# A new order for the first stage of an attention kernel with two feed-forward blocks: pieces, ring places and PSUM banks

## The chip, the cores and the metric

The kernel runs on one core of a Trainium2 chip. The metric is the device time of one execution in microseconds (us); for the kernel before it is the median of three runs. Beside these stands one profiled execution, whose trace is read below.

## What is computed

From `q`, `k`, `v` of shape (4, 8, 576, 64), all float32, attention is computed within chunks of 64 positions; its result, as 2304 tokens by 512, goes through two feed-forward blocks of width 2048.

```python
scores = scale * np.matmul(q_c, k_c.transpose(0, 1, 2, 4, 3))     # chunks of 64
attn = softmax(scores); out = np.matmul(attn, v_c)
x = out.transpose(0, 2, 1, 3).reshape(2304, 512)
r = np.maximum(x @ w_in, 0.0); x = (s * (r * r) + b) @ w_out       # first block
h = x @ w_in2; return (h * np.tanh(softplus(h))) @ w_out2           # second block
```

## The kernel before

The 2304 tokens are 18 tiles of 128, grouped in five blocks of 512, 512, 256, 512 and 512 tokens. The feed-forward width is cut into 16 chunks of 128, four to a group. The kernel has a first stage, which does the attention of all 18 tiles and the first group (four chunks) of the first block, and then a long second stage, in which loops go over the remaining groups of both blocks. Matmuls are done in two words (high and low parts of each number), three products for one.

The first stage is written out by hand as one string, `START`. Each word is a piece, and the pieces are issued in that order; a piece goes to the queue of its engine, so that each engine meets its own pieces in the order of the string. A word is a name, the index of a tile, weight or step, after a dot the place in an SBUF ring, and after @ the PSUM banks. The names that matter here:

- Loads, all on SP's queue: `dq`, `dk`, `dv` bring a tile of q, k or v (256 KB each; tiles 4 and 13 come as two halves). `W` brings a 512 KB weight: 0, 1, 3, 5 are the input weights of chunks 0 to 3, and 2, 4, 6, 7 their output weights. `sb` brings two scalars. From tile 8 on, q and k share a ring of six places: a load into a place waits until TensorE has read what lay there.
- TensorE (PE in the profile): `K` and `Q` transpose a loaded tile (4 matmuls, L248); `S` makes the scores (L271, 32 rows in the profile); `T` transposes the softmax (L248); `X` multiplies with v (L313). `I` and `J` are the two halves of a feed-forward input product (6 matmuls each, L342), `O` and `P` those of an output product (L378). There are 20 feed-forward steps, four for each block. `w5@6` issues five matmuls of zeros (L459; ten rows in the profile) into a bank: filler.
- ScalarE (ACT) and VectorE (DVE): `k`, `q`, `t` copy a transposed tile out of PSUM (ACT); `m`, `e`, `n`, `z` are the softmax; `x`, `y` split the attention's output in two words; `a`, `c`, `d`, `h`, `l` decode a weight; `r`, `u`, `v`, `g`, `o` are the activation. `E` takes a finished sum out of banks 0 to 3 (on ACT for the first sum of a block, L388). `F` and `G` prepare the second stage.

```python
for w in START.split():
    name, i, m, bank = re.fullmatch(r"([a-zA-Z]+)(\d*)(?:\.(\d))?(?:@(\d+))?", w).groups()
    pieces(name, int(i or 0), int(m or 0), int(bank or 0))
```

Of the kernel before, what the change touches and what calls it, by code (L numbers as in the profile page):

```python
# [21 lines left out]
NS = 4  # L22

START = (
# [26 lines left out]
)  # L51

PAIRS = ((0, 1), (3, 4))
# [1406 lines left out]
```

## Time and profile before

| What | us |
|---|---|
| median of 3 runs (lowest, highest) | 814.95 (814.93, 816.12) |
| the profiled execution's own time | 818.31 |
| its span, first to last instruction | 816.5 |
| PE busy in the span | 798.9 (98%) |
| DVE busy, ACT busy | 656.8 (80%), 499.8 (61%) |

The profiled execution has 1.8 us around its span and took 3.4 us more than the median. "Busy" of PE includes filler, and a matmul counts as busy also while the clock is low. Where PE is not busy, the timeline names in brackets how long it stood and what ended the wait.

### The profile page before, as it was taken

Reading aid. Unit: us, or ns where it says so; the run is one execution under the profiler, and the core shown is the slowest. Engines: PE = TensorE matmul, PEld = TensorE weight load, DVE = VectorE, ACT = ScalarE, POOL = GpSimd, SP = SyncE. Lnnn points to the kernel's source line nnn. Section 1 sums busy time; section 2 is a strip of 40 time slices with the busy share of each in tenths; the row PEclk is TensorE's granted clock in tenths of the full one; section 3 lists DMA queues with packets and bytes.
Section 4 is the critical chain, followed back from the end, with each engine's and each line's share of the span. In section 5 each row is a group of like instructions: output and inputs, shape, how many; then the busy total and the mean of one; then the engine's idle time right before and its main releaser. Section 6 shows DMA issues by size and latency. Waiting matters only on the chain.

```text
span 816.5 us, 13885 instructions
## 1 busy us (share of the span) xinstructions
PE 798.9 (98%) x5482; PEld 696.1 (85%) x5482; DVE 656.8 (80%) x1174; ACT 499.8 (61%) x905; POOL 0.7 (0%) x7
## 2 busy tenths in 40 slices
PE   7879999999999999999999999999999999999998
PEld 6767888888888888888888888899899998998997
DVE  5778899968776697757987796899969999889774
ACT  4769767776657486644767364767446563746460
POOL 0000000000000000000000000000000000000000
PEclk9999999999999999999999999999999999999999
DMA  8999622197596543855156440877655757545522
GB/s 199 215 236 264 212 64 81 72 339 259 157 379 240 203 156 140 324 208 204 52 188 243 193 201 3 318 302 255 221 206 192 275 189 261 186 172 212 194 86 104
DMA packets 102049, 163.43 MB, mean 200 GB/s; under 512 B 60000, under 2 KB 80480, under 8 KB 92256
## 3 DMA queue, kind: packets, MB, share of 16 engines
q1 hardware_dynamic: 101984, 162.55, 57.9%
q8 instruction: 43, 0.70, 0.4%
q14 instruction: 22, 0.18, 0.1%
HBM read 127.40 MB, written 35.13 MB: 199 GB/s over the span
## 4 chain that ended last, share of the span: by engine, by line
PE 90%; SPq 4%; DMA 3%; ACT 1%; DVE 1%; issue 0%; DVEq 0%
PE ps L955 38%; PE ps L378 29%; PE ps L987 17%; PE ps L342 5%; SPq L240 3%; DMA qk<-in_k_dram 1%; DMA wraw<-in_moe_w_in_dram 1%; PE ps L248 1%; DMA qk<-in_q_dram 1%; PE ps L313 1%; DVE wdec L158 0%; PE ps L271 0%; ACT ysum L388 0%; ACT wdec L158 0%; ACT r L471 0%
## 5 line engine op out<-in xcount | busy, mean ns | idle before, releaser
L378 PE MATMUL ps<-ghi,w 128*128 128x512 f32 (+1 forms) x512 | 130.0, 371 | 0.0
L955 PE MATMUL ps<-xs,wx 128*128 128x512 f32 (+1 forms) x516 | 121.9, 376 | 0.0
L378 PEld LDWEIGHTS ps<-ghi,w 128*128 128x128 f32 x512 | 91.3, 189 | 15.9
L955 PEld LDWEIGHTS ps<-xs,wx 128*128 128x128 f32 x516 | 90.4, 189 | 15.5
L955 PE MATMUL ps<-xs,w 128*128 128x512 f32 (+1 forms) x384 | 89.3, 370 | 0.0
L158 DVE SCALAR_TENSOR_TENSOR wdec<-wraw,wdec 128x512 uint32<-128x512 uint32 x128 | 87.2, 688 | 1.8
L955 PEld LDWEIGHTS ps<-xs,w 128*128 128x128 f32 x384 | 67.2, 189 | 11.5
L378 PE MATMUL ps<-glo,w 128*128 128x512 f32 (+1 forms) x256 | 75.1, 369 | 0.0
L955 PE MATMUL ps<-xs,wb 128*128 128x512 f32 x288 | 74.6, 391 | 0.0
L158 DVE TENSOR_SCALAR wdec<-wdec 128x512 f32<-128x512 f32 (+1 forms) x128 | 53.3, 423 | 15.9 <-ACT wdec L158 14.8
L955 PEld LDWEIGHTS ps<-xs,wb 128*128 128x128 f32 x288 | 52.7, 188 | 9.8
L1004 DVE TENSOR_TENSOR ysum<-ps,ysum 128x512 f32<-128x512 f32 x76 | 51.4, 687 | 11.7 <-PE ps L987 11.2
L399 DVE TENSOR_TENSOR ysum<-ps,ysum 128x512 f32<-128x512 f32 (+1 forms) x66 | 39.9, 638 | 23.8 <-PE ps L378 23.8
L378 PEld LDWEIGHTS ps<-glo,w 128*128 128x128 f32 x256 | 46.9, 188 | 8.3
L1119 ACT COPY ur<-ps 128x512 f32<-128x512 f32 x40 | 23.5, 587 | 43.2 <-PE ps L955 40.8
L342 PE MATMUL ps<-xhi,w 128*128 128x512 f32 (+1 forms) x160 | 46.7, 375 | 0.0
L987 PE MATMUL ps<-wc,rm 128*128 128x256 f32 x312 | 44.4, 282 | 0.0
L987 PEld LDWEIGHTS ps<-wc,rm 128*128 128x128 f32 x312 | 41.6, 191 | 1.4
L378 PE MATMUL ps<-gr,w 128*128 128x512 f32 (+1 forms) x192 | 42.6, 363 | 0.0
L158 DVE TENSOR_TENSOR w<-wdec,w 128x512 fp32r<-128x512 f32 x50 | 34.2, 686 | 9.9 <-ACT w L158 9.9
L1119 ACT COPY ps<-ps 128x512 f32<-128x512 f32 (+1 forms) x56 | 29.0, 521 | 19.8 <-PE ps L987 10.2
L378 PEld LDWEIGHTS ps<-gr,w 128*128 128x128 f32 x192 | 33.4, 189 | 5.7
(210 smaller groups left out, 1616.6 us busy)
## 6 DMA issues: line engine op xcount, KB each, us to landing
wraw<-in_moe_w_in_dram SPq DMA_DIRECT2D x32, 512.0 KB, 5.7
wraw<-in_moe_w_out_dram SPq DMA_DIRECT2D x32, 512.0 KB, 5.3
xs<-d20t SPq DMA_DIRECT2D x12, 1024.0 KB, 5.1
xs<-d23t SPq DMA_DIRECT2D x12, 1024.0 KB, 4.7
xs<-d13b SPq DMA_DIRECT2D x9, 1024.0 KB, 6.1
xs<-d20b SPq DMA_DIRECT2D x9, 1024.0 KB, 4.9
xs<-d23b SPq DMA_DIRECT2D x9, 1024.0 KB, 6.2
xs<-d10t SPq DMA_DIRECT2D x8, 1024.0 KB, 7.4
```

What stands on the lines that cost most here:

```text
L158: ins = issue(**z)
L240: nc.sync.dma_start(out=t[o:o + n].rearrange("p (h d) -> p h d", h=H), in_=dict(k=k, q=q, v=v)[which][bb, :, ss:ss + n, :].rearrange("h s ...
L248: nc.tensor.transpose(out=p[:, a], in_=src[:, a * P:(a + 1) * P], identity=ident)
L313: nc.tensor.matmul(out=xp[j * CH:(j + 1) * CH, c, a, :], lhsT=at["v", i][r, h * CH:(h + 1) * CH], rhs=at["pt", i][r, 2 * ap + a2, g:g + CH],)
L342: nc.tensor.matmul(out=hp, lhsT=w[:, sl], rhs=r[b][:, a, :], start=(a == 0 and p == 0), stop=(a == KD - 1 and p == 2),)
L378: nc.tensor.matmul(out=acc[m][:, :n] if l == 1 else acc[m], lhsT=w[wi][:, sl] if l == 1 else g[gi][:, sl], rhs=g[gi] if l == 1 else w[wi], ...
L399: nc.vector.tensor_tensor(out=y, in0=a[:, :w], in1=y, op=ALU.add)
L955: nc.tensor.matmul(out=out, lhsT=w[i][:, a * P:(a + 1) * P], rhs=x[j][:, a], start=(begins and a == 0 and p == 0), stop=(ends and a == KD ...
L987: nc.tensor.matmul(out=bank[:, t * n:(t + 1) * n], lhsT=g[u][x][:, (2 * j + t) * P:(2 * j + t + 1) * P], rhs=w[u][y], start=False, stop=(u ...
L1004: nc.vector.tensor_tensor(out=z, in0=bank.rearrange("p (t d) -> p t d", d=n), in1=z, op=ALU.add)
L1119: nc.scalar.copy(out=out, in_=i)
```

## The change

The string `START` is replaced. The pieces are the same apart from the filler: 17 calls of a zero matmul before (in four words), 23 after (in ten). What differs is their order, the ring places and the banks. The first line and its replacement:

```diff
-    "dk2 W0 dq2 w5@6 K2@0 dk3 dq3 a0 k2.0 dq0 w5@6 Q2@0 c0 dk0 dk6 K3@4 dk5 q2.0 dk1 d0 S2@67 k3.1 Q3@2 dq5 dq1 h0 "
...
+    "dk1 w5@6 K1@6 dq1 Q1@4 W0 k1.0 dk3 dq3 q1.0 dq0 w1@6 S1@23 m1.4 a0 e1 c0 n1 d0 w3@6 K3@4 k3.1 w2@6 Q3@1 dq2 w2@6 "
...
```

The loads alone, in queue order up to the k tile 12, and then PE's pieces up to the transposes of that tile:

```
loads before: dk2 W0 dq2 dk3 dq3 dq0 dk0 dk6 dk5 dk1 dq5 dq1 dq6 dq4 dq15 dq9 dk9 dv2 dk10 dk7 dq7 dv3 dv0 dk4 dv1
              dq12 dq8 W1 dq10 dv5 dk17 sb dv6 dk8 dk16 dv7 dk11 dq11 dv4 dq14 dq16 dk12
loads after:  dk1 dq1 W0 dk3 dq3 dq0 dq2 dk0 dk2 dq9 dk6 dq6 dq5 dk5 dv1 dv3 dk9 dv0 dk4 dq4 dv2 W1 dq7 dq10 dk7 dv5
              dk10 dk8 dv6 dq8 dv7 dq11 dv4 dk12 | sb W3 dk11 W2 dv9 dq12 dq16 W5 dk15 dk13
PE before: w5 K2 w5 Q2 K3 S2 Q3 Q0 S3 K0 w2 S0 w5 Q5 K1 K5 K6 T2 Q1 Q6 S1 Q4 T3 S6 Q15 K9 X2 S5 Q9 K10 K7 T0 S9 X3
           Q7 T1 X0 K4 T6 S7 X1 S4 Q12 Q8 I0 T5 Q10 J0 K17 S10 X6 X5 K8 K16 I3 T4 J3 T7 K11 X4 S8 X7 Q14 Q11 K12
PE after:  w5 K1 Q1 w1 S1 w3 K3 w2 Q3 w2 Q0 S3 Q2 w2 K0 w2 K2 S0 T1 Q9 S2 w3 Q6 w2 Q5 K6 K5 S6 w1 T3 T0 S5 X1 K9 T2
           X0 S9 K4 Q4 X3 X2 T5 S4 I0 J0 Q7 K7 T6 Q10 X5 S7 K10 I3 J3 K8 Q8 X6 S10 T7 T4 Q11 X7 X4 S8 T9 K12
```

On SP's queue the change shows at the k tile 12. Before, the rows from the v tile 6 (`v_86`) to the k tile 12, the last row (rows of 64 are half tiles):

```order
L240 DMA v_86<-in_v_dram 128x8x64
L240 DMA qk<-in_k_dram 128x8x64 x2
L240 DMA v_86<-in_v_dram 128x8x64
L240 DMA qk<-in_k_dram 128x8x64
L240 DMA qk<-in_q_dram 128x8x64
L240 DMA v_86<-in_v_dram 64x8x64 x2
L240 DMA qk<-in_q_dram 128x8x64 x2
L240 DMA qk<-in_k_dram 128x8x64
```

After, from the v tile 6 to the k tile 12 and on to the weight `W3`:

```order
L240 DMA v_86<-in_v_dram 128x8x64
L240 DMA qk<-in_q_dram 128x8x64
L240 DMA v_86<-in_v_dram 128x8x64
L240 DMA qk<-in_q_dram 128x8x64
L240 DMA v_86<-in_v_dram 64x8x64 x2
L240 DMA qk<-in_k_dram 128x8x64
L438 DMA s_sb<-in_moe_s_dram 128x1
L439 DMA b_sb<-in_moe_b_dram 128x1
L146 DMA wraw<-in_moe_w_in_dram 128x4x256
```

Four q and k loads stood between the v tiles 6 and 4 and two q loads between the v tile 4 and the k tile 12; now it is two and none, and the two scalars come behind the k tile 12.

On PE at the same tile, before: the transposes of the q tiles 14 and 11, the k tile 12 and the q tile 16 in one row (x16), then those of the softmax of tile 9 (`e`) and the product `I2` on the second block's tokens:

```order
L248 MATMUL ps<-ident,e_87 128x128 x4
L248 MATMUL ps<-ident,qk 128x128 x4
L313 MATMUL ps<-room,v_86 64x64 x16
L271 MATMUL ps<-kt,qt 64x64 x16
L313 MATMUL ps<-room,v_86 64x64 x16
L248 MATMUL ps<-ident,qk 128x128 x16
L248 MATMUL ps<-ident,e 128x128 x4
L342 MATMUL ps<-xhi_701,w 128x512 x2
```

After: the last row of transposes from `qk` is that of the k tile 12; in front stand the products of tiles 7 and 4 with v, the scores of tile 8 and the softmax of tile 9, behind it `I1`:

```order
L248 MATMUL ps<-ident,e_87 128x128 x8
L248 MATMUL ps<-ident,qk 128x128 x4
L313 MATMUL ps<-room,v_86 64x64 x32
L271 MATMUL ps<-kt,qt 64x64 x16
L248 MATMUL ps<-ident,e 128x128 x4
L248 MATMUL ps<-ident,qk 128x128 x4
L342 MATMUL ps<-xhi_621,w 128x512 x2
```

The transposes of the q tiles 14 and 16 have moved behind the k tile 12, and the softmax of tile 9 in front of it.

## Rows read from the trace of the kernel before

**Rows 1.** Busy time by stretch: each engine's us and count, PE's clock, DMA share, GB/s.
```profile
0.00:20.00 20.00, 15.09 (x168) 13.11 (x169) 10.10 (x20) 8.25 (x13) 0.74 (x7) 0.95 0.85 199
20.00:40.00 20.00, 17.72 (x402) 15.05 (x400) 15.50 (x31) 14.51 (x27) 0.00 (x0) 0.97 0.95 222
40.00:60.00 20.00, 15.01 (x266) 12.63 (x265) 15.51 (x31) 13.77 (x26) 0.00 (x0) 1.00 0.89 225
60.00:80.00 20.00, 20.00 (x217) 16.39 (x216) 16.38 (x33) 17.55 (x33) 0.00 (x0) 1.00 0.97 254
80.00:100.00 20.00, 18.32 (x244) 15.27 (x243) 16.51 (x32) 15.71 (x30) 0.00 (x0) 1.00 0.76 251
100.00:171.60 71.60, 71.60 (x595) 60.73 (x594) 67.74 (x113) 52.75 (x100) 0.00 (x0) 1.00 0.28 96
171.60:816.50 644.90, 641.13 (x3600) 562.96 (x3598) 515.04 (x918) 377.28 (x680) 0.00 (x0) 1.00 0.57 207
```

**Rows 2.** PE's waits over the span: us in total, times, longest.
```profile
PE ps L248 <- DMA qk<-in_q_dram: 4.1, 4, 2.4
PE ps L248 <- DMA qk<-in_k_dram: 4.0, 6, 1.5
PE ps L313 <- DMA v<-in_v_dram: 1.7, 1, 1.7
PE ps L248 <- ACT kt L256: 1.2, 2, 0.6
PE ps L271 <- ACT ysum L388: 1.1, 1, 1.1
```

**Rows 3.** Timeline of PE: start, length, what, count, idle before; filler and early stops.
```profile
1.05 2.50 PE L459 MATMUL ps<-zero 128*128 128x128 f32 x10 [1.05 <-DVE zero L863]
...
4.67 2.34 PE L459 MATMUL ps<-zero 128*128 128x128 f32 x10
...
13.78 1.38 PE L459 MATMUL ps<-zero 128*128 128x128 f32 x10
17.53 3.30 PE L248 MATMUL ps<-ident,qk 128*128 128x128 f32 x16 [2.36 <-DMA qk<-in_q_dram]
```

**Rows 4.** Timeline of PE, the later stops for a load, and what follows the last.
```profile
34.17 0.63 PE L248 MATMUL ps<-ident,qk 128*128 128x128 f32 x4 [0.81 <-DMA qk<-in_k_dram]
...
41.19 0.63 PE L248 MATMUL ps<-ident,qk 128*128 128x128 f32 x4 [1.04 <-DMA qk<-in_q_dram]
...
45.94 1.16 PE L313 MATMUL ps<-room,v 64*64 64x64 f32 x64 [1.67 <-DMA v<-in_v_dram]
...
49.16 0.63 PE L248 MATMUL ps<-ident,qk 128*128 128x128 f32 x4 [1.46 <-DMA qk<-in_k_dram]
...
57.28 1.06 PE L248 MATMUL ps<-ident,qk 128*128 128x128 f32 x8 [0.82 <-DMA qk<-in_k_dram]
...
60.01 0.62 PE L342 MATMUL ps<-xhi,w 128*128 128x512 f32 x2
...
61.38 0.62 PE L342 MATMUL ps<-xhi,w 128*128 128x512 f32 x2
```

**Rows 5.** Timeline of PE: the two last stops of the first stage, and its end.
```profile
81.30 0.66 PE L248 MATMUL ps<-ident,room 128*128 128x128 f32 x4 [0.59 <-ACT kt L256]
...
86.54 1.17 PE L271 MATMUL ps<-kt,qt 64*64 64x64 f32 x60 [1.09 <-ACT ysum L388]
...
171.39 0.61 PE L955 MATMUL ps<-xhi,w 128*128 128x512 f32 x2
```

**Rows 6.** Timeline of ACT: the weight W3 is awaited.
```profile
61.03 0.66 ACT L158 ACTIVATE wdec<-wraw 128x512 f32<-128x512 f32 x1 [0.61 <-DMA wraw<-in_moe_w_in_dram]
```

**Rows 7.** SP's waits before loads, between 30 and 60 us, by what ended them.
```profile
SPq L240 <- PE ps L248: 4.4, 4, 1.9
```

**Rows 8.** Busy time by stretch: after the longest stop, and around the scalars.
```profile
16.00:18.00 2.00, 0.47 (x4) 0.48 (x5) 1.26 (x4) 0.00 (x0) 0.00 (x0) 0.99 0.33 77
18.00:20.00 2.00, 2.00 (x12) 2.00 (x11) 0.55 (x1) 1.12 (x2) 0.00 (x0) 0.50 0.97 219
20.00:22.00 2.00, 2.00 (x14) 2.00 (x13) 1.67 (x5) 1.07 (x2) 0.00 (x0) 0.65 1.03 232
22.00:24.00 2.00, 1.71 (x43) 1.40 (x42) 0.41 (x1) 1.56 (x3) 0.00 (x0) 1.00 0.89 203
...
42.00:44.00 2.00, 2.00 (x38) 1.52 (x40) 1.93 (x4) 1.69 (x4) 0.00 (x0) 1.00 0.21 35
```

50 rows, old and new, of the table START are left out of this document.

## The prediction, made before the change was run

> **What bounds the kernel now.** I first read the busy time by stretch [rows 1]. From 100 us to 171.6 us PE is busy without a break, and then it is busy almost to the end: what it loses there is the 3.8 us of the last output. Its only other holes are in the first 100 us: 4.91, 2.28 and 4.99 us in the first three stretches of 20 us, none in the fourth, 1.68 us in the fifth. The order of one string can only move these holes, the filler and the time at a low clock; PE's real work is the same, and nothing behind 171.4 us, where the second stage begins [rows 5], has slack to give back or take up.
>
> Next come PE's waits [rows 2]. Those for loads of q, k and v are 9.8 us together. Two others count, both on ACT: the copy of a k tile and the eviction of a sum, 0.59 and 1.09 us at 81 and 87 us [rows 5]; they are the 1.68 us above. DMA is 85 to 97% busy up to 80 us and 28% from 100 us [rows 1]. So the first 60 us are paced by loads, the rest by PE, and the place where the one gives way to the other is the last stop for a load: at 57.28 us, 0.82 us long, in front of the transposes of the k tile 12 (`K12`) [rows 4].
>
> The timeline gives a ladder of landings, since a stop that a load ends shows when it landed. I number the loads by what stands in the queue up to and with them (256 KB a tile, 512 KB a weight, the scalars nothing). Before, the q tile 5 is at 3.0 MB and lands at 17.5 us [rows 3]; the k tile 4 is at 6.25 MB, 34.2 us; the q tile 10 at 7.75 MB, 41.2 us; the v tile 6 at 8.5 MB, 45.9 us; the k tile 16 at 9.0 MB, 49.2 us; the k tile 12 at 10.75 MB, 57.3 us [rows 4]; the weight `W3` at 11.75 MB, 61.0 us [rows 6]. The same kinds of loads stand in the same queue afterwards, so I take the ladder over.
>
> **The change, term by term.** The time of the first stage's end is the time of the last load stop, plus PE's work behind it, plus stops behind it.
>
> First, the load. The k tile 12 moves from 10.75 MB to 9.0 MB in the queue: it is the 36th unit of 256 KB instead of the 43rd. By the ladder it lands at 49.16 instead of 57.28 us [rows 4]: -8.1 us. The next load that could bind is the k tile 13, at 12.0 MB, that is shortly after 61.0 us, about 61.8. Between `K12` and `K13` PE has 12.9 us of work in the new order (`K12 K11 T10 Q12` at 0.53, `S11` and `X9` at 0.58, and `I1 I2 J1 J2 I4 I6 J4` at 1.37 each, prices that follow in a moment), so it comes there at about 62.0 us: just no stop.
>
> Second, the work behind `K12`. Prices: a piece of four transposes 0.53 us (eight in 1.06), an `X` 0.58 (two in 1.16), an `S` the same, half a product 1.37 us (from 60.01 to 61.38) [rows 4]; a zero matmul 0.28 us (five calls in 1.38) [rows 3]. With `K12` itself, four `K`, three `Q` and ten `T` stood at or behind it; now seven `K`, six `Q` and nine `T`. `S`, `X`, `I`, `J`, `O`, `P` are as many as before and filler is at neither place. That is five more transposes: +2.65 us.
>
> Third, the two stops of 0.59 and 1.09 us [rows 5]. The first stands before `T12`, which took the bank of `K14` before the copy was out; now `T12` takes the bank of `K17` with `T13`, `Q14`, `J7`, two `S` and an `X` between, over 4 us: gone. The second stands before `S14`, which came one `X` behind the end of a sum that ACT had to evict; now the first user of these banks comes one `X` and one `K` behind, and each needs one bank only. I leave 0.5 us for it: -1.1 us; all of it gone would be -1.7, none of it 0.
>
> The sum is -8.1 + 2.65 - 1.1 = -6.55 us. On the profiled execution's own 818.31 us (its span is 816.5) that makes 811.8; the median of the runs was 3.4 us below that execution, and the same difference on 814.95 gives 808.4 us.
>
> **Does PE get to K12 in time?** This is the uncertain step. Ahead of 49.16 us PE now has more to do. Before, the pieces ahead of the stop at 49.16 were 12 `K`, 13 `Q`, 10 `S`, 6 `T`, 6 `X`, one `I` and `J` and 17 zero matmuls; ahead of `K12` in the new order are 11, 12, 11, 9, 8, two `I` and `J` and 23. That is one transpose piece (0.53), an `S` and two `X` (1.74), `I` and `J` (2.74) and six fillers (1.7): +6.7 us. The holes up to there were 4.91 + 2.28 + 4.99 - 0.82 = 11.4 us [rows 1, 4]. One thing comes back: after the stop of 2.36 us [rows 3] the granted clock was 0.50 and 0.65 for two stretches of 2 us [rows 8], which is 1.0 + 0.7 = 1.7 us of PE lost; with filler in ten places and tiles 2, 0 and 9 to work on around 3.0 MB I expect no stop of that length. So PE is in time if the holes ahead of `K12` fall from 11.4 to 6.4 us. I think they do, for these reasons. The 2.36 us stop stood where only filler was ahead of the load at 3.0 MB. The stops at 7.75, 8.5 and 9.0 MB (1.04, 1.67, 1.46 us) stood where the second input weight `W1` came at 7.5 MB and its products `I3`, `J3` therefore after 49 us; now it is at 6.0 MB and they stand ahead of the load at 8.5 MB. If none of the holes went, `K12` would begin 5.0 us later, at 54.2.
>
> The ends of the first term follow. Upper: 54.2 us, -3.1. Lower: part of the ladder was made by SP, which waited 4.4 us for ring places [rows 7], and by the two scalars; around them DMA was 21% busy for 2 us [rows 8], a hole of 1.6 us. In the new order each place of the q and k ring has been read when SP comes to it, and the scalars come behind the k tile 12: 47.6 us, -9.7.
>
> The Trainium skill, "TensorE: Matmul & The Clock Gate", Part 1, speaks against the start of the new order: the throttled state is the default and activity releases it, and at the first filler only one zero matmul follows now where five did. The trace has both sides: the ten rows of the second filler took 2.34 us and the same ten 1.38 us later [rows 3]. By the rows alone the start costs the same; by the rule it could cost as in the rival on the clock.
>
> **Rivals.** *The holes stay.* `K12` is bound by PE instead of by its load, the first term is -3.1 and the sum -1.55: 813.4 us. For it: DVE and ACT are three quarters busy from 20 us on [rows 1], and many short waits for a copied bank add up; the new order uses banks more tightly at `K9`, `S9`, `X3`. Against it: the largest holes are all loads.
>
> *The clock stays low at the start.* If it is at the lower of its levels (1.2 of 2.4 GHz) until 3.0 MB, the nine pieces from `K3` to `T1` cost about 0.55 us more each, 5 us; the holes that stood there, 2.36 us [rows 3] and some shorter ones, take up about 3 us of it, and `K12` begins 2 us late: 810.4 us. Against: at 13.78 us the filler was already fast [rows 3], with little work in between.
>
> *More than forecast.* SP never waits and the ladder is 1.6 us shorter up to 9.0 MB, and both later stops go: -9.7 + 2.65 - 1.7 = -8.7 us, 806.2 us. Against: `K13` must then be earlier as well.
>
> *Slower than before.* ACT works in order, and `a5` waits for the weight `W5`, with the copies `t10`, `q12` and `k13` behind it; PE needs the bank of `T10` for `Q16`, at about 62.6 us. By the ladder `W5`, at 11.5 MB, lands at 60.1 us, 1.2 us before it matters (two ACT operations of 0.6). Each us beyond 61.3 is a us of PE, so the kernel is slower than before by 0.2% from a landing at about 69.5 us; at 71.3 us it takes 818.4 us. For it: ACT did stand 0.61 us for a weight, `W3` [rows 6]. Against: no landing on the ladder is 8 us off its neighbours.
>
> **How the numbers follow.** A difference of 0.2%, 1.6 us, is about what a measurement of this kernel can tell from none. Chances: the forecast with its neighbourhood (806.5 to 811.5, the clock's rival within it at 0.08) 0.72; more than forecast 0.07; the holes stay 0.16, a little over half of that within 0.2%; slower 0.05. So faster 0.85, same 0.10, slower 0.05. The range goes from 805.0, just below the lower end of the terms, to 813.4, their upper end. I predict 808.4 us.
>
> **What would show it.** `K12` begins at 49 us without or with a short stop; the holes in the first 49 us are 6 to 7 us; no stretch of 2 us after 8 us has a granted clock below 0.9; no stop for a load comes after `K13`; the matmuls of the second stage (L955) begin at about 165 us instead of 171.4, and the rest of the span is unchanged. I am wrong if `K12` begins well after 50 us with waits on ACT or DVE in front, if `W5` or the k tile 13 lands after 62 us, or if the second stage shows holes that it did not have.

## The result and the profile after

| What | before | after |
|---|---|---|
| median of 4 runs each (lowest, highest), us | 815.47 (814.93, 816.12) | 808.87 (808.05, 809.01) |
| ratio, 95% interval | | 0.9917 [0.9899, 0.9934] |
| the profiled execution's own time, us | 818.31 | 808.96 |
| its span, us | 816.5 | 807.2 |

The changed kernel is faster by 6.6 us (0.8%). The number is almost the predicted one; the road to it isn't. (The interval leaves out 1, so the difference is clear, small as it is.)

The busy time of PE by stretch in the profile of after (us, PE's busy time and count, PE's clock, DMA share, GB/s), which answers to [rows 1]:

```profile
0.00:20.00 20.00, 17.97 (x227) 1.00 0.91 214
20.00:40.00 20.00, 18.35 (x396) 1.00 0.98 229
40.00:60.00 20.00, 19.15 (x312) 1.00 0.85 210
60.00:80.00 20.00, 18.95 (x217) 1.00 0.99 275
80.00:100.00 20.00, 20.00 (x288) 1.00 0.73 236
100.00:165.00 65.00, 65.00 (x476) 1.00 0.40 148
165.00:807.20 642.20, 638.35 (x3588) 1.00 0.56 203
```

PE's holes in the first five stretches are 2.03, 1.65, 0.85, 1.05 and 0 us, where they were 4.91, 2.28, 4.99, 0 and 1.68. The granted clock reads 1.00 in every stretch (for the first microseconds see the run without filler below), and the stretches behind are as before: no hole up to 165 us and 3.85 us at the end. PE's waits for loads (us, times, longest), which answer to [rows 2]:

```profile
PE ps L248 <- DMA qk<-in_k_dram: 1.2, 2, 0.9
```

Loads of q and v are gone from the list, and of those of k 1.2 us is left. The timeline of PE in after shows where, beside the end of the first stage, for [rows 4, 5]:

```profile
45.82 0.60 PE L248 MATMUL ps<-ident,qk 128*128 128x128 f32 x4
...
59.52 1.09 PE L248 MATMUL ps<-ident,qk 128*128 128x128 f32 x8 [0.85 <-DMA qk<-in_k_dram]
...
65.78 0.65 PE L248 MATMUL ps<-ident,qk 128*128 128x128 f32 x4 [1.04 <-ACT r L354]
...
161.98 0.62 PE L955 MATMUL ps<-xhi,w 128*128 128x512 f32 x2
```

The transposes of the k tile 12 (`K12`, 45.82) wait for nothing. The last stop for a load is now in front of those of the k tile 13 (`K13`, 59.52, 0.85 us). A new stop of 1.04 us stands before `Q13`, 65.78, and is ended by ACT. The second stage begins at 161.98 us, 9.41 us earlier than in the profile of before. From there to the end of the execution both take the same: 818.31 - 171.39 = 646.92 and 808.96 - 161.98 = 646.98 us. In all thirteen profiles of this document it is 646.9 to 647.4 us. So the start of the second stage is a direct reading of an execution's time, and I use it as such below.

For the load itself, the view of DMA issues (tile, engine, count, KB, us from issue to landing) for the issue at 41.21 us:

```profile
qk<-in_k_dram SPq DMA_DIRECT2D x1, 256.0 KB, 3.2
```

The k tile 12 lands at about 44.4 us and PE uses it 1.4 us later.

### The profile page after: what moved, and what is told of

Same layout as the page of the kernel before. It is cut to its first block, busy times and chain, and to the rows that moved or that the text cites. A ratio compares the mean times of both kernels' runs of the same rounds, so it can differ in the third digit from the quotient of the medians.

```text
span 807.2 us, 13907 instructions
## 1 busy us (share of the span) xinstructions
PE 797.8 (99%) x5494; PEld 695.4 (86%) x5494; DVE 655.7 (81%) x1174; ACT 498.8 (62%) x905; POOL 0.7 (0%) x7
## 4 chain that ended last, share of the span: by engine, by line
PE 95%; DVE 2%; DMA 1%; ACT 1%; SPq 0%; issue 0%; DVEq 0%
PE ps L955 38%; PE ps L378 30%; PE ps L987 17%; PE ps L342 5%; PE ps L248 2%; PE ps L271 1%; PE ps L313 1%; DMA wraw<-in_moe_w_out_dram 1%; SPq L240 0%; DVE mx L277 0%; DVE e L278 0%; DMA qk<-in_k_dram 0%; DVE sm L289 0%; DVE wdec L158 0%; ACT e L285 0%
## 5 line engine op out<-in xcount | busy, mean ns | idle before, releaser
L1004 DVE TENSOR_TENSOR ysum<-ps,ysum 128x512 f32<-128x512 f32 x76 | 51.5, 689 | 11.7 <-PE ps L987 11.4
L987 PE MATMUL ps<-wc,rm 128*128 128x256 f32 x312 | 44.4, 282 | 0.0
```

The costliest lines, as they stand in the source:

```text
L987: nc.tensor.matmul(out=bank[:, t * n:(t + 1) * n], lhsT=g[u][x][:, (2 * j + t) * P:(2 * j + t + 1) * P], rhs=w[u][y], start=False, stop=(u ...
L1004: nc.vector.tensor_tensor(out=z, in0=bank.rearrange("p (t d) -> p t d", d=n), in1=z, op=ALU.add)
```

## The experiments

All of them run beside the kernel before, whose medians were 815.92, 816.24 and 814.72 us in the three groups; ratios are to that. Each time is a median with the lowest and highest run.

### The same two kernels once more

**The kernel before, unchanged** (first group).

> The kernel before, unchanged, profiled once more. The profiled execution of before took 3.3 us more than the median of its runs, while the profiled one of the changed kernel sits on its median; so between the two traces 9.3 us of span separate the kernels, between the medians 6.6 us. First theory: the execution in the first trace had an unluckily long stop at the load at 3.0 MB (2.36 us) and the low clock behind it; then this trace has a shorter stop there, no stretch with a granted clock of 0.5, the stop in front of K12 at about 54 to 55 us instead of 57.3, and a span of about 813 to 814 us. Rival: a profile lengthens the kernel before by 3 us as a rule; then this trace looks like the first one, with a span of 816 us and the stop at 57 us. In both the ratio to before is 1.000 within 0.002.

815.99 us (813.2 to 818.5), ratio 0.9993 [0.9978, 1.0008]. Its timeline of PE, for [rows 3 to 5]:

```profile
16.10 1.99 PE L248 MATMUL ps<-ident,qk 128*128 128x128 f32 x16 [1.79 <-DMA qk<-in_q_dram]
...
56.27 1.91 PE L248 MATMUL ps<-ident,qk 128*128 128x128 f32 x8 [1.98 <-DMA qk<-in_k_dram]
...
171.34 0.61 PE L955 MATMUL ps<-xhi,w 128*128 128x512 f32 x2
```

The long stop at 3.0 MB is 1.79 instead of 2.36 us and no low clock follows it; another stop, of 1.46 us, stands at 24.75 us that the first profile did not have; `K12` begins at 56.27 instead of 57.28, and it is here that the granted clock falls (eight transposes take 1.91 us, where they took 1.06). Yet the second stage begins at 171.34, as before. So the ladder of landings is no property of the kernel: it differs by 1 to 3 us between executions of the same code, and the profile of before was one from the upper side of a spread of 813 to 819 us. The first theory had the shorter stop right and the rest wrong. Its rival, that a profile lengthens this kernel, is not refuted: the profiled 818.50 us is the longest of these twelve runs.

**The kernel after, unchanged** (third group).

> The changed kernel, unchanged, timed once more on the chip of the two that follow and profiled. Forecast: 808 to 810 us, 0.991 to 0.993 of before; in this trace PE comes to K12 without a stop or with one under 0.5 us, between 45 and 48 us, and no stretch ahead of 60 us has a granted clock under 0.9. Rival (the first trace was a lucky one): stops for loads between 30 and 50 us and a low clock behind one of them, 811 us.

808.96 us (806.41 to 810.78), ratio 0.992 [0.9898, 0.9942]. The view of DMA issues shows the load of the k tile 12, issued at 38.82 us, and the timeline of PE `K12`, `K13` and the second stage:

```profile
qk<-in_k_dram SPq DMA_DIRECT2D x1, 256.0 KB, 4.0
```

```profile
45.56 0.60 PE L248 MATMUL ps<-ident,qk 128*128 128x128 f32 x4
...
59.37 1.09 PE L248 MATMUL ps<-ident,qk 128*128 128x128 f32 x8 [0.94 <-DMA qk<-in_k_dram]
...
161.97 0.62 PE L955 MATMUL ps<-xhi,w 128*128 128x512 f32 x2
```

The load lands at about 42.8 us, 1.6 us earlier than in the first profile of after, but `K12` begins only 0.26 us earlier, `K13` waits 0.94 us for its load, and the second stage begins within 0.02 us of the first profile. What the load of the k tile 12 gains is worth nothing any more: it has stopped being what PE waits for.

### Where the load stands

**The change with the load of the k tile 12 put back.**

```diff
- ... Q10@5 dk12.1 sb n9 ...  m10.1 dq12.3 z9 ...
+ ... Q10@5 sb n9 ...  m10.1 dk12.1 dq12.3 z9 ...
```

It stands then at 10.5 MB by the ladder's count, 0.25 MB ahead of its place in before (the expectations below have it at 10.75); PE's order is that of after.

> The changed kernel with one load moved: the k tile 12 back from 9.0 to 10.75 MB in the queue, where it stood before. PE's order is untouched. In the trace of the changed kernel the load that would then stand ahead of it (the v tile 9) lands at 52.3 us, so the tile lands at about 53.2 us, and PE, which comes to K12 at 45.8 us, stops for 7.4 us. Behind K12 stand 12.9 us up to K13, whose own stop of 0.85 us goes: load theory 6 to 6.6 us slower than the changed kernel, 814.5 to 815.5 us. Rival: the stop lets ACT and DVE catch up, the stop of 1.04 us for a copy at 65.8 us goes too and other short waits with it: 4 to 5.5 us slower, 812.5 to 814.5 us.

816.78 us (815.28 to 818.61), ratio 0.9997 [0.9984, 1.001]: the whole gain is lost. Its timeline of PE, and its busy time by stretch (PE, weight loads, DVE, ACT, POOL, clock, DMA share, GB/s):

```profile
30.25 1.07 PE L248 MATMUL ps<-ident,qk 128*128 128x128 f32 x4 [2.99 <-DMA qk<-in_q_dram]
...
55.01 1.11 PE L248 MATMUL ps<-ident,qk 128*128 128x128 f32 x4 [5.59 <-DMA qk<-in_k_dram]
55.77 1.20 PE L342 MATMUL ps<-xhi,w 128*128 128x512 f32 x2
...
61.03 0.62 PE L342 MATMUL ps<-xhi,w 128*128 128x512 f32 x2
...
171.56 0.61 PE L955 MATMUL ps<-xhi,w 128*128 128x512 f32 x2
```

```profile
54.00:56.00 2.00, 0.99 (x5) 0.99 (x6) 0.00 (x0) 0.00 (x0) 0.00 (x0) 0.54 0.70 156
56.00:58.00 2.00, 2.00 (x6) 1.57 (x6) 0.61 (x2) 1.84 (x4) 0.00 (x0) 0.50 0.92 259
```

PE is done with everything ahead at 49.4 us and stands 5.59 us for the load. The clock falls while it stands, and the matmuls behind run at the lower level (two rows of 128x512 products take 1.05 us between, 0.62 once it is back at 61.03). This profile has a second long stop, 2.99 us at 30.25 us, with a granted clock of 0.57 and 0.58 in the two stretches of 2 us from 30 us on. That costs PE some 1.7 us, but PE then stands at `K12` for longer than that: this low clock lies ahead of a load stop that covers it. The same kernel in the third group, on the chip on which the unchanged kernel after took 808.96 us:

> The changed kernel with the k tile 12 at 10.75 MB, as in the earlier run of that edit; on one chip with the kernel that has filler in its stop, since the first two were timed on different chips. 1.000 of before within 0.0015.

815.72 us (813.81 to 816.92), ratio 1.0005 [0.9994, 1.0015], 6.8 us above after. In the new order the place of this one load is worth as much as the whole change. It is not enough by itself, as the next run shows.

**The reverse: the kernel before with this load early.**

```diff
- ... sb t6.0 dv6 X1@56 y0 dk8.1 S4@01 ... Q12@7 Q8@4 ... I3@6 k16.3 dk12.1 z4 ...
+ ... sb t6.0 X1@56 y0 S4@01 ... Q12@7 dk12.4 dv6 dk8.1 Q8@4 ... I3@6 k16.3 z4 ...
```

The ring places of the k tile 11 and the q tiles 11, 14 and 16 move with it; PE's order is that of before.

> The kernel before with the load of the k tile 12 moved from 10.75 to 8.5 MB in the queue (ring places of four other loads change with it); PE's order is that of before. Forecast's shorthand taken literally (the place of this load is worth its 8 us): 808 us. Rival (the first term needs PE's new order as well: before, the loads for X6 and K16 bind just ahead of K12, and PE's work between stops leaves it there at 56.5 us or later): the stop at K12 goes, those at X6 and K16 become 0.9 us longer, and the time is 814.5 to 816.5 us.

816.43 us (815.02 to 818.6), ratio 1.0006 [0.9994, 1.0019]: nothing. Its timeline of PE:

```profile
45.01 1.16 PE L313 MATMUL ps<-room,v 64*64 64x64 f32 x64 [2.60 <-DMA v<-in_v_dram]
...
47.15 2.00 PE L248 MATMUL ps<-ident,qk 128*128 128x128 f32 x8 [0.98 <-DMA qk<-in_k_dram]
...
55.39 1.97 PE L248 MATMUL ps<-ident,qk 128*128 128x128 f32 x16
...
169.68 0.62 PE L955 MATMUL ps<-xhi,w 128*128 128x512 f32 x2
```

`K12`, in the row of 16 at 55.39, waits for nothing. But the v tile 6, now behind, is late (2.60 us), and from 47.15 us on PE is the bound in its old order. The stop at `K12` was only 0.82 us long [rows 4] (1.98 us in the second profile of before): that is all that the load by itself could give back. It is worth 7 us only together with an order in which PE is there earlier.

### The clock and the filler

**The kernel before with more filler ahead of the load at 3.0 MB.**

```diff
- ... S0@67 w5@4 Q5@5 m0.6 ...
+ ... S0@67 w5@4 w8@4 Q5@5 m0.6 ...
```

> The kernel before with eight more zero matmuls behind the filler at 13.78 us, so that PE works through the stop of 2.36 us and its clock stays up. Load theory (what counts is the last stop for a load; time won ahead of it is lost again at the next load): the granted clock stays at 1.00 between 16 and 22 us, the 1.7 us are lost again at the loads that follow, and the time is that of before within 0.8 us. Clock theory (the low clock behind the stop is part of what the new order won): 1.5 to 2.5 us faster than before.

816.35 us (814.66 to 818.26), ratio 0.9999 [0.9985, 1.0013]. Timeline of PE, and its busy time by stretch:

```profile
12.82 3.17 PE L459 MATMUL ps<-zero 128*128 128x128 f32 x26
16.29 0.87 PE L248 MATMUL ps<-ident,qk 128*128 128x128 f32 x6 [0.31 <-DMA qk<-in_q_dram]
...
24.40 0.63 PE L248 MATMUL ps<-ident,qk 128*128 128x128 f32 x4 [1.59 <-DMA qk<-in_k_dram]
...
55.01 1.06 PE L248 MATMUL ps<-ident,qk 128*128 128x128 f32 x8 [0.59 <-DMA qk<-in_k_dram]
```

```profile
24.00:26.00 2.00, 1.45 (x49) 0.92 0.69 157
26.00:28.00 2.00, 2.00 (x37) 0.50 1.07 243
28.00:30.00 2.00, 2.00 (x28) 0.72 1.02 232
```

The 26 rows of filler leave a stop of only 0.31 us at 3.0 MB. The clock stays up there and falls 8 us later instead, at 26 us, after the next stop. Some 2 x (0.08 + 0.50 + 0.28) = 1.7 us of PE are lost there, as much as in the first profile of before, and stops for loads come behind, of which the last is the one at 55.01. So filler in front of this stop doesn't show in the time. What it would be worth to have no low clock at all this run doesn't say, since the clock only fell at another place.

**The change without 18 of its 23 zero matmuls** (all but the first word are left out; no result depends on them).

```diff
- ... dq0 w1@6 S1@23 ... d0 w3@6 K3@4 k3.1 w2@6 Q3@1 dq2 w2@6 Q0@6 ...
+ ... dq0 S1@23 ... d0 K3@4 k3.1 Q3@1 dq2 Q0@6 ...
```

> The changed kernel without its filler, except the first word of five zero matmuls: 18 calls out of 23 are left out. Load theory: the filler stands where PE would wait, so the stops grow by its 5 us and the end stays, within 0.8 us of the changed kernel (808 to 810 us). Clock theory: PE's clock falls to 0.5 in some stretch before 24 us and the pieces there take twice as long; K12 and K13 begin late, and it takes 811 to 814 us.

808.62 us (807.32 to 810.74), ratio 0.9902 [0.9881, 0.9924]. Its timeline of PE, and behind it a row of scores from that of after:

```profile
8.51 2.93 PE L248 MATMUL ps<-ident,qk 128*128 128x128 f32 x12 [0.94 <-DMA qk<-in_k_dram]
11.36 1.13 PE L271 MATMUL ps<-kt,qt 64*64 64x64 f32 x32
...
160.64 0.62 PE L955 MATMUL ps<-xhi,w 128*128 128x512 f32 x2
```

```profile
10.82 0.69 PE L271 MATMUL ps<-kt,qt 64*64 64x64 f32 x32
```

The granted clock reads 1.00 in every stretch here too, but the rows say otherwise. Twelve transposes in 2.93 us are as slow as the eight in 1.91 us at 56.27 us in the second profile of before, where the granted clock was low, and the scores take 1.13 us for 0.69. So without the filler TensorE runs at the lower level until about 13 us; in after it is at speed before 8.4 us. At the start of an execution the clock's column misses this. The slow rows cost over 2 us of PE, and the median doesn't show it. But the 18 zero matmuls that are left out, 5 us of PE, went with them, so the run doesn't price the low clock alone. The new filler does nothing for the time.

**Filler in front of the late load.** To the change with the load put back, 18 zero matmuls:

```diff
- ... T9@2 dk15.5 K12@3 k12.3 ...
+ ... T9@2 dk15.5 w18@3 K12@3 k12.3 ...
```

> The changed kernel with the k tile 12 at 10.75 MB again, and 18 zero matmuls in front of K12 on PE, 5 us of filler in a stop that took 5.6 us in the trace of the kernel without them. There the granted clock was 0.5 for 6.8 us behind the stop, which is 3.4 us of PE. Clock theory (a low clock behind the last load stop is paid in full, unlike one ahead of it): no low clock there, 2.5 to 3.5 us faster than that kernel, 813.3 to 814.3 us. Rival: behind the stop PE waits for copies anyway, so nothing is won: 816 to 817 us.

815.2 us (813.27 to 818.46), ratio 0.9995 [0.9981, 1.0009]. Against the kernel without that filler (0.9997), no difference, but that ran on another chip, so both were run again on one:

> The same with 18 zero matmuls in front of K12. Clock theory: 2.5 to 3.5 us faster than the kernel without them on the same chip, about 0.997 of before. Rival: under 1 us of difference; the low clock is then not what the late load costs, or the filler takes back what it saves when the load lands early.

813.32 us (811.26 to 816.2), ratio 0.9986 [0.9969, 1.0002]; without the filler 815.72 us, ratio 1.0005 [0.9994, 1.0015]. The timelines of PE: filler in the first pair, filler in the second, and the second without filler:

```profile
46.48 4.18 PE L459 MATMUL ps<-zero 128*128 128x128 f32 x36
52.50 0.66 PE L248 MATMUL ps<-ident,qk 128*128 128x128 f32 x4 [1.83 <-DMA qk<-in_k_dram]
...
166.25 0.62 PE L955 MATMUL ps<-xhi,w 128*128 128x512 f32 x2
```

```profile
46.61 4.18 PE L459 MATMUL ps<-zero 128*128 128x128 f32 x36
52.71 0.66 PE L248 MATMUL ps<-ident,qk 128*128 128x128 f32 x4 [1.92 <-DMA qk<-in_k_dram]
...
54.11 1.05 PE L342 MATMUL ps<-xhi,w 128*128 128x512 f32 x2
...
168.07 0.62 PE L955 MATMUL ps<-xhi,w 128*128 128x512 f32 x2
```

```profile
54.32 1.12 PE L248 MATMUL ps<-ident,qk 128*128 128x128 f32 x4 [6.27 <-DMA qk<-in_k_dram]
...
169.96 0.62 PE L955 MATMUL ps<-xhi,w 128*128 128x512 f32 x2
```

From `K12` to the second stage PE takes 113.75 us where the clock stayed up (first pair), and 115.36 with filler and 115.64 without in the second, 116.55 without in the first. So a low clock behind the last load stop costs 1.6 to 2.8 us of these executions, and filler prevented it in one of two. Why only in one is not shown: the filler ran out at 50.7 and 50.8 us, and PE stood 1.83 and 1.92 us, almost the same. `K12` itself came 2.5 and 1.6 us earlier in the two filler executions, because its load landed earlier; the profiled executions without filler were the longest of their kernel's runs both times. The mean granted clock of every run is on record and tells more than two profiles. Without the filler it is 0.993 to 0.996 in all 23 runs. With it, it is at least 0.999 in 11 of 24; these have medians of 814.3 and 812.6 us in the two groups, and the other 13 have 816.3 and 815.6 us, about as without filler. So the filler goes with 2 to 3 us where the clock stayed up, in about half of the runs, and with nothing in the others.

### The new stop, and a better version

**`a5` behind `q12`.** ACT meets its pieces in the order of the string, and `a5` waits for the weight `W5` (1.92 us in the profile of after). Moved behind the copy of the q tile 12:

```diff
- ... J4 a5 K13@1 ... t10.1 c5 q12.0 ...
+ ... J4 K13@1 ... t10.1 q12.0 a5 c5 ...
```

> The changed kernel with one piece of ACT moved: a5, which waits for the weight W5 and in the trace of the changed kernel held ACT for 1.92 us at 58 us, now stands behind e11, t10 and q12, which need no load. Theory (the stop of 1.04 us at 65.8 us comes from this wait, handed on through g3 and r2 to the bank of Q13): ACT works through most of the wait, the stop goes, and the kernel is up to 1.0 us faster than the changed one, 808 us. Rival: the stop is only the end of a chain with slack elsewhere, or the weight lands at another time in other executions; then it is the same within 0.5 us. Both are near the limit of what can be told; the trace decides by whether the stop at Q13 is there.

809.62 us (808.36 to 811.73), ratio 0.993 [0.991, 0.9949]. The stop before `Q13` is gone and the second stage begins at 161.49 us, but stops of 0.32 and 0.58 us stand at 50.89 and 53.50 us instead; the time is that of after. That the move of `a5` took the stop away is likely and not shown by this profile alone: in that of the run without 18 zero matmuls, with `a5` in its old place, `W5` came in time (ACT decodes it at 56.73 us without waiting), and the stop is missing too.

**The same, with the load of the k tile 13 in front of `W5` and the k tile 15.**

> The same, and the two halves of the k tile 13 are moved ahead of W5 and the k tile 15 in the queue, since their load ended the last load stop of the changed kernel (0.85 us at 59.5 us). If the end is set by the last load stop, both stops go and it takes about 807 us, 1.5 to 1.9 us less than the changed kernel. Rival: with both stops gone PE is bound by its own work from 30 us on only in some executions, and W5, 0.9 us later, hands its lateness on: 808 to 809 us.

809.17 us (807.64 to 811.01), ratio 0.9924 [0.9905, 0.9943]. Its timeline of PE:

```profile
29.18 0.63 PE L248 MATMUL ps<-ident,qk 128*128 128x128 f32 x4 [1.75 <-DMA qk<-in_q_dram]
...
59.64 1.04 PE L248 MATMUL ps<-ident,qk 128*128 128x128 f32 x8
...
161.83 0.62 PE L955 MATMUL ps<-xhi,w 128*128 128x512 f32 x2
```

`K13` and `Q13` wait for nothing, but in this execution a load at 29.18 us was late by 1.75 us, and PE comes to `K13` at 59.64 us, 0.12 us later than in after. The second stage begins at 161.83 us. With the stop at `K13` removed, PE's work from that late load on is the bound in this execution, and the late load costs as much. Both edits stand in this run together, so it says nothing on one of them alone. I found no version that beats the change.

## Why the prediction came out right, step by step

**The first term, the load: the cause right, the size and the binding load wrong.** I had `K12` bound by its load at 49.16 us, -8.1. It begins at 45.82 us, -11.46 in the profiled pair, and waits for nothing. Two things were wrong in that step. First, I took the ladder over from one execution, and the load at 9.0 MB came at 46.65 us in the second profile of before and at 44.4 and 42.8 us in the two of after. In these the hole in DMA traffic that stood behind the scalars, a DMA share of 0.21 at 42 to 44 us in before [rows 8], stands behind the k tile 12 (0.32 at 44 to 46 us in the first), as my lower bound had it. Secondly, I set the last load stop at `K12` and called `K13` "just no stop". My price list put PE at `K13` 12.9 us behind `K12`; it came there 12.85 us behind (59.52 - 0.85 - 45.82). But I had its load at 61.8 us and PE at 62.0, a margin of 0.2 us between two numbers that both were off by 2 to 3 us (by the ladder's own last step, 3.7 us for 1.0 MB, the load would have stood at 62.0). It landed at about 59.5 us, PE was there at 58.67, and the stop is 0.85 us; in the run without 18 zero matmuls it is missing. That the load's place is a cause was right: put back, it costs 6.8 us on the same chip.

**PE in time at `K12`: right, with room.** I needed the holes ahead of it to fall from 11.4 to 6.4 us. The busy time of PE in after, by stretch from the start to `K12` and from there to the second stage, columns as in the first fence:

```profile
0.00:45.82 45.82, 42.15 (x806) 1.00 0.91 210
45.82:161.98 116.16, 114.26 (x1090) 1.00 0.61 189
```

The holes ahead are 45.82 - 42.15 = 3.67 us, and the work there 42.15 us, near the 42.8 that I reckoned with. The rival in which the holes stay is out. The kernel before with the load alone moved shows that this step is as much a condition as the load's place: either alone gives nothing.

**The second term, work behind `K12`: right in sign, 0.8 us too large.** Before, from 57.28 to 171.39, it was 114.11 - 1.68 = 112.43 us without the two stops; now it is 114.26: +1.83 us where I had +2.65. Why the five transposes cost less than their price is not shown.

**The third term, stops behind `K12`: wrong.** The stops of 0.59 and 1.09 us [rows 5] did go, as argued. But two others came, 0.85 us at `K13` and 1.04 us at `Q13`: +0.21 us instead of -1.1. The second is the mechanism of my slower rival at a small size. Timeline of ACT in after:

```profile
58.06 0.66 ACT L158 ACTIVATE wdec<-wraw 128x512 f32<-128x512 f32 x1 [1.92 <-DMA wraw<-in_moe_w_in_dram]
...
63.58 0.66 ACT L158 ACTIVATE wdec<-wraw 128x512 f32<-128x512 f32 x1 [0.51 <-DMA wraw<-in_moe_w_out_dram]
...
65.14 0.59 ACT L354 ACTIVATE r<-ps 128x512 f32<-128x512 f32 x1
```

ACT stands 1.92 us for `W5` (58.06) and 0.51 us for the next weight (63.58); the eviction at 65.14 comes late by that, and `Q13` needs its bank. I had worked out the price at another bank user, `Q16`, and set it at nothing below a landing of 61.3 us; `W5` landed at 58.0 us and it cost 1 us all the same. In the second profile of after ACT stands 2.39 us for `W5`, and the stop is 1.22 us.

**The sum, and the correction to the median.** In the profiled pair the terms measured -11.46 + 1.83 + 0.21 = -9.42 us, against -6.55 forecast, and the two executions' own times differ by 9.35 us. The medians differ by 6.60. I had carried the 3.4 us by which the profiled execution of before lay above its median over to the kernel after; but that one's profiled execution lies 0.1 us from its median. So two errors of about 3 us cancel, and that the sum came within half a us of the median is luck in this respect: the first term was too small for the profiled pair, and the offset did not carry over. By the median instead, an estimate: a time of 815 us puts the second stage at 815 - 647 = 168 us and `K12` at 168 - 114.1 = 54 us, so that to 45.82 the first term is about -8 us. It fits the forecast of -8.1, but for an execution whose ladder I had not seen.

**The clock's rival: false.** I gave 0.08 to a low clock up to 3.0 MB. By the lengths of its rows TensorE is at speed before 8.4 us in after, with one zero matmul where five were; without 18 of the 23 it is so only from about 13 us on, and the median stays the same. The Trainium skill, "TensorE: Matmul & The Clock Gate", Part 1, by which the throttled state is the default and activity releases it, would let one expect a slow start where filler is thin. The trace agrees, and no more than that: the slow start is there and has no price here. **"More than forecast"** has its mechanism (landings earlier than the ladder) in the trace and not its time, since `K13` then binds, as I held against it. Of the signs I named, those for `K12` (49 us), the holes ahead (6 to 7 us) and the second stage (165 us) were missed on the early side, at 45.82, 3.67 and 161.98 us; no load stop came after `K13` and no low clock after 8 us.

**Open:** why executions of the kernel before scatter by 5 us and their loads by 1 to 3, and what the low clock costs it: in the three groups its runs with a mean granted clock of at most 0.997 have medians 0.9 to 1.9 us above those with at least 0.999, but where in them the clock fell is not on record. Open is also whether profiled executions of kernels that wait for loads lie above their medians as a rule. They lie 3.4 and 2.5 us above for the two of before, 1.8 and 1.2 for the two with the load put back, 0.6 with the load early, 0.4 with filler in before, and -1.9 and +1.7 with filler in front of the late load. Those of after and of the three kernels derived from it that hardly wait lie between 1.0 us below and 0.1 us above.

## What to carry to other kernels

The length of the stop at a load (0.82 and 1.98 us here) is all that an earlier load gives by itself; what it allows together with an order in which PE comes earlier can be several times as much (6.8 us here), so cost the two together, and look for the next load that binds with the margin of the ladder in mind. A ladder of landings read from one execution has an error of some us: set no "just no stop" on 0.2 us of it, and check whether the profiled execution lies beside its median before carrying an offset over. In this kernel a low clock was paid for behind the last load stop; a longer load stop behind it covered it, and filler ahead of an earlier one bought nothing.

## What was not expected of the hardware

The same program's loads land at different times from one execution to the next: the k tile 12 of the kernel after at about 44.4 and 42.8 us, and `K12` of the kernel before begins at 57.28 and 56.27 us. With them the place moves at which the granted clock falls: at 18 us [rows 8] and at 56 us in two executions of the kernel before, at 26 us with filler, at 47 us with the load early, and nowhere behind the start in those of after, whose longest stop behind the start is 1.04 us in the first profile and 1.22 us in the second. At the start the clock's column reads 1.00 while rows take about twice as long as later (eight transposes 1.94 us at 3.81 us without 18 zero matmuls, 1.06 us at 22.47 us); in that run this lasts to about 13 us, in after it is over before 8.4 us.
